# Placing anew the FFT pieces, PSUM banks and operand sums of a fused Fourier-mixing and MLP kernel

## The chip, the cores and the metric

The kernel runs on one core of a Trainium2 chip. The metric is the device time of one execution in microseconds (us); of several executions the median is taken. Five engines work at once, each through its own list of instructions: TensorE (PE) multiplies, VectorE (DVE) and ScalarE (ACT) work element by element, GpSimd (POOL) and SyncE (SP) mostly issue DMA transfers here. An instruction that must wait holds up all that stands behind it on its engine.

## The reference

Eight sequences of 3008 tokens by 256 channels are filtered in the frequency domain, and each token then goes through an MLP with a parametric ReLU.

```python
X = np.fft.rfft(x, axis=1)                  # x: (8, 3008, 256)
Y = X * (filt_r + 1j * filt_i)[None]        # 1505 frequencies x 256
y = np.fft.irfft(Y, n=3008, axis=1).reshape(24064, 256)

h = y @ moe_w_in                            # 256 -> 2048
g = np.maximum(h, 0.0) + moe_alpha * np.minimum(h, 0.0)
return g @ moe_w_out                        # 2048 -> 256, float32
```

## The kernel before

**The Fourier part.** 3008 is 47 x 64, and each transform is done as two small transforms with twiddle factors between them, all as matmuls in fp16. Per batch there are four kinds of pieces:

- 16 a pieces (`piece_a`, matmul at L211): x, loaded in four chunks by GpSimd (L170), against a 47-point table; ScalarE takes the result to `asb`, and SyncE stores it to DRAM (L216) and reads it back transposed as `at` (`turn_a`).
- 12 b pieces (`piece_b`, L231): two matmuls of 256 columns into one PSUM bank; VectorE multiplies that bank twice with the filter, into `ww` (L234) and `uu` (L235), and two DMAs of GpSimd add the halves of `ww`, swapped, onto `uu` (L237).
- 12 c pieces (`piece_c`, L249): two matmuls of `uu`, which ScalarE takes to `v` (L281). After every third one `turn_c` has SyncE write `v` to DRAM in four DMAs (L258); after the last it also issues the first three loads of the transposed `zt` (L267).
- 16 d pieces (`piece_d`, L274): four matmuls of 94 columns from `zt`, which ScalarE takes to `yT`, the MLP's input.

The first batch is done before the main loop with other, wider pieces; only 12 of its turns (`piece_t`, L352) and 12 of its d pieces are spread over the loop's start. Its filter multiplications use a filter without the sign and swap that later batches need; these are made in the loop by `neg` on VectorE (L626) and by `swapped` on GpSimd's DMA queue (L630).

All pieces of the later batches share two PSUM banks, the tiles `psF`. The string `BANKS` has one digit for each piece, in the order in which they are issued, and says which of the two it takes. A piece can only start when its bank has been emptied by the engine that reads the earlier piece in it.

**The MLP.** Batches are taken in four pairs. A pair has twelve blocks, eleven of 512 tokens and one, the sixth, of 384, so there are 48 blocks. A block has 16 steps; `step` is 16 x block + j. A step does, in this order: `flush()` (what the last block's end left to VectorE and SyncE), the operand sums due at this step (`ahead`), the pieces due at it (`plan`), `settle()` (VectorE's second half of the activation, L685), `blk.up(j)` (two matmuls of 512 columns for one 128-wide slice of the hidden layer, L498; after each second one ScalarE copies 1024 columns to `gtb`, L506, and VectorE forms the negative part, L509), and as many down matmuls of the blocks before as `LAG` lets through. So everything on TensorE is in one hand-made order, and the down products of block n run from step 16n + 18 on.

A plain block (`eight()`, L537) does 16 matmuls of 256 columns for each 128 tokens, evicts with ScalarE (L542) and stores with SyncE (L467). A block in `FAST` (`seven()`, L559) does its 2 x 2 block product with seven multiplications in place of eight: 112 matmuls of 128 columns, seven to each step. They need sums of the hidden layer's quarters a11, a12, a21, a22 and of the weights. `combine` makes the weights' sums once, at `STEPS_K`, into `tw_s` (L669 to L677). The hidden layer's are made by `Block.sums(w, h)`, h being the first or the second half of the slices:

- w = 1: z1 = a21 + a22, on VectorE (L518), into `ss`
- w = 2: z2 = z1 + a11, on VectorE (L520)
- w = 3: a21 += a11, by an accumulating DMA of GpSimd (L524, `gtb<-gtb` in the profile)
- w = 4: a12 += z2, by such a DMA (L524, `gtb<-ss`)
- w = 5 and w = 6: what 3 and 4 do, but by VectorE (L526)

Each entry of `SUMS` and `TAIL` is (step after 16n, w, h). A fast block uses `SUMS` if it lies before block 39 and the block ahead of it in order is plain, and `TAIL` otherwise. The products come in the order a12, a11, a22, z2, z1, a21, a12; the sixth begins near 16n + 29.4, the last, which reads a12 + z2, near 16n + 31.7.

**The steps.** `STEPS_A` to `STEPS_D` give the steps of the pieces of the batches from 4 on, counted from 96 (b - 1); `FIRST` gives them for batches 1 to 3. `STEPS_T` and `STEPS_E` are the first batch's turns and d pieces, `STEPS_F` and `STEPS_N` the swaps and negations of the filter, `STEPS_K` the weights' sums, `STEPS_X` and `STEPS_Q` the loads of x.

Of the kernel before, what the change touches and what calls it, by code (L numbers as in the profile page):

```python
# [19 lines left out]
DFF = 2048  # L20
NH = 32
BANKS = (
    "010101010101010101010101010101001010010110010010101010101010100101001010010101010101010100101010"
    "101010101010101010101001010101001011010101011010110110101101010101010101101001011010101101010010"
    "101101010011010101101010101010101010110010101010101101001000101001010101010101010101010101010110"
    "101010101011010010010101101010101010101010101010101010010101101010110100100010100101010101010101"
    "01010101010101101010101101001110101010101010101010101010"
)
STEPS_A = (-84, -81, -77, -76, -65, -59, -58, -58, -56, -53, -52, -51, -50, -48, -46, -43)
STEPS_B = (-21, -15, 4, 6, 13, 21, 25, 27, 32, 40, 54, 55)  # L30
STEPS_C = (2, 10, 16, 19, 24, 33, 35, 46, 62, 63, 70, 70)
STEPS_D = (89, 89, 90, 91, 92, 94, 95, 98, 100, 101, 105, 113, 118, 125, 144, 147)
STEPS_T = (0, 0, 2, 2, 13, 17, 19, 21, 21, 35, 40, 43)
STEPS_E = (6, 6, 7, 11, 23, 27, 29, 29, 53, 54, 55, 56)
STEPS_N = (24, 29, 35, 40)
STEPS_F = (20, 16, 22, 28, 34)
STEPS_K = (118, 121, 128, 133, 144)
STEPS_X = ((20, 27, 42, 52), (107, 109, 113, 126))
STEPS_Q = (-28, -18, -8, -3, 1, 9, 15, 23)
FIRST = (  # L40
# [12 lines left out]
)  # L53
FAST = frozenset((8, 10, 12, 14, 16, 18, 20, 22, 24, 26, 28, 30, 32, 34, 36, 38, 40, 42, 43, 44, 45))
SUMS = ((9, 1, 0), (10, 3, 0), (16, 2, 0), (17, 1, 1), (17, 3, 1), (19, 2, 1), (20, 4, 0), (21, 6, 1))
TAIL = ((13, 1, 0), (13, 3, 0), (18, 1, 1), (18, 3, 1), (18, 2, 0), (18, 2, 1), (20, 4, 0), (21, 4, 1))
LAG = 17
AF = mybir.ActivationFunctionType
OP = mybir.AluOpType

# [41 lines left out]
def kernel(  # L102
# [377 lines left out]
    class Block:  # L480
        def __init__(self, n, p, t0, tn):
            self.n, self.p, self.t0, self.tn = n, p, t0, tn
            self.fast = n in FAST
            self.sent = 0
# [132 lines left out]
    def put(step, fn, *args):  # L617
        plan.setdefault(step, []).append((fn, args))

    for i in range(12):  # L620
        ev = both[i % 2] if i < 4 else (on_dve, on_act)[i // 8]
        put(STEPS_T[i], f0.piece_t, 4 + i, ev)
        put(STEPS_E[i], f0.piece_d, 4 + i, ev)

# [6 lines left out]

    put(STEPS_F[0], lambda: nc.gpsimd.dma_start(out=twi_s[64:128], in_=twx_s[64:128]))
    for i in range(4):
        put(STEPS_F[1 + i], swapped, 6 * i, 6 * i + 6)
        put(STEPS_N[i], neg, 6 * i, 6 * i + 6)
    for b in range(1, NB):
        p = 96 * (b - 1)
        f = Fft(b)
        steps_a, steps_b, steps_c, steps_d = FIRST[b - 1] if b < 4 else (STEPS_A, STEPS_B, STEPS_C, STEPS_D)
        for i in range(16):  # L640
# [3 lines left out]
        if b + 1 < NB:  # L644
            for c in range(4):
                if b < 3:
                    put(STEPS_X[b - 1][c], load_x, b + 1, c)
                else:
                    for h in range(2):
                        put(p + STEPS_Q[2 * c + h], load_x, b + 1, c, (h,))  # L650
        quarters, later = (4, 1) if b < 3 else (1, 4)
# [27 lines left out]
    for n in range(5):  # L679
        put(STEPS_K[n], combine, n)  # L680
    owed = []
# [8 lines left out]
    for n, (p, t0, tn, _) in enumerate(blocks):  # L690
        old, blk = blk, Block(n, p, t0, tn)
        if blk.fast:
            for at, w, h in SUMS if n < 39 and n - 1 not in FAST else TAIL:
                ahead.setdefault(16 * n + at, []).append((blk, w, h))
        for j in range(16):
# [9 lines left out]
            blk.up(j)  # L705
            while todo and done < (step - LAG) / 16:
                try:
# [41 lines left out]
```

## Time and profile before

| what | us |
|---|---|
| median of 3 runs | 778.01 |
| lowest and highest of them | 777.71, 780.72 |
| own time of the profiled execution | 778.49 |
| its span in the profile | 776.7 |
| PE busy | 759.6 (98%) |
| VectorE busy | 691.0 (89%) |
| ScalarE busy | 606.1 (78%) |
| GpSimd busy | 264.7 (34%) |

The profile has one row for each group of instructions: line and engine, operation, written and read tiles with their shapes, the count, then busy time and mean duration, then the idle time just before them and what ended it. A row of the timeline has the start and the length of one or several instructions in a row, and in brackets the idle time ahead of them and what released them. A matmul's end in the trace is modelled, so rows of TensorE overlap; its starts are measured.

### The profile page before, as it was taken

How to read it: one execution, taken by the hardware profiler on the slowest of the kernel's cores; microseconds unless marked ns; L12 is line 12 of the kernel's file. 1: busy time of each engine (PE TensorE's matmuls, PEld its weight loads, DVE VectorE, ACT ScalarE, POOL GpSimd, SP SyncE). 2: the span in 40 equal slices, each digit the busy share in tenths (PEclk: the TensorE clock that was granted, in tenths of full speed). 3: DMA queues.
4: the chain of work that ended last, by engine and by line, in shares of the span. 5: the costliest groups of instructions: out<-in, count | busy, mean ns of one | idle time of the engine just before them, and what ended most of it. 6: DMA issues, size and time to landing. Idle time of an engine off the chain costs nothing.

```text
span 776.7 us, 18287 instructions
## 1 busy us (share of the span) xinstructions
PE 759.6 (98%) x6952; PEld 541.9 (70%) x6952; DVE 691.0 (89%) x1517; ACT 606.1 (78%) x902; POOL 264.7 (34%) x351
## 2 busy tenths in 40 slices
PE   7899999999999999999999999999999999999998
PEld 6756667666676767766677767767677777777776
DVE  3788996799999999999899999989999999989994
ACT  4687678888788887888878888788878777787773
POOL 6830641144234342353233422434222333103210
PEclk9999999999999999999999999999999999999999
DMA  9996858666997679886797869966786645635642
GB/s 181 191 191 185 163 110 209 185 130 138 192 201 153 125 162 189 207 151 129 162 196 151 156 136 178 210 134 131 161 191 153 127 86 103 167 84 105 129 96 68
DMA packets 112879, 118.74 MB, mean 153 GB/s; under 512 B 12616, under 2 KB 94296, under 8 KB 112792
## 3 DMA queue, kind: packets, MB, share of 16 engines
q0 software_dynamic: 32656, 47.99, 38.4%
q1 hardware_dynamic: 79992, 69.52, 33.7%
q8 instruction: 54, 0.88, 0.5%
q14 instruction: 33, 0.27, 0.1%
q10 hardware_dynamic: 144, 0.07, 0.0%
HBM read 56.06 MB, written 46.66 MB: 132 GB/s over the span
## 4 chain that ended last, share of the span: by engine, by line
PE 87%; DVE 4%; DMA 4%; ACT 3%; issue 1%; POOL 1%; SPq 1%; DVEq 0%; ACTq 0%; POOLq 0%
PE hps L498 38%; PE op L537 20%; PE op L559 16%; PE psF L211 3%; PE psF L274 3%; PE psF L249 2%; PE psF L231 2%; ACT gtb L506 2%; DMA twf_s<-c_twf 1%; DVE m L509 1%; DVE gtb L685 1%; DMA zt<-v_dram 1%; PE op L592 1%; DVE ww L234 1%; DVE uu L235 1%
## 5 line engine op out<-in xcount | busy, mean ns | idle before, releaser
L506 ACT ACTIVATE gtb<-hps 128x1024 f16<-128x1024 f32 (+1 forms) x384 | 385.9, 1005 | 110.5 <-PE hps L498 106.5
L498 PE MATMUL hps<-yT,win_s 128*128 128x512 f16 (+1 forms) x1536 | 449.2, 374 | 0.0
L509 DVE TENSOR_SCALAR m<-gtb,alm_s 128x512 f16<-128x512 f16 (+1 forms) x768 | 235.1, 348 | 45.4 <-ACT gtb L506 43.7
L685 DVE TENSOR_TENSOR gtb<-gtb,m 128x1024 f16<-128x1024 f16 (+1 forms) x384 | 260.9, 679 | 14.2
L537 PE MATMUL op<-wout_s,gtb 128*128 128x256 f16 x1600 | 243.1, 272 | 0.0
L237 POOL DMA_DIRECT2D uu<-ww x168 | 142.2, 1014 | 263.1 <-DVE uu L235 165.2
L537 PEld LDWEIGHTS <-gtb 128*128 128x128 f16 x1600 | 156.0, 98 | 104.6
L498 PEld LDWEIGHTS <-win_s 128*128 128x128 f16 x1536 | 136.7, 98 | 25.6 <-issue 2.5
L559 PEld LDWEIGHTS <-gtb 128*128 128x128 f16 x1680 | 114.3, 98 | 53.8 <-DMA gtb<-ss 1.0
L524 POOL DMA_DIRECT2D gtb<-gtb x42 | 40.5, 963 | 192.9 <-DVE ss L518 62.1
L559 PE MATMUL op<-wout_s,gtb 128*128 128x128 f16 x1008 | 85.1, 219 | 1.1 <-ACT gtb L506 0.6
L281 ACT ACTIVATE asb<-psF 96x512 f16<-96x512 f32 x112 | 65.1, 594 | 9.7 <-PE psF L211 8.4
L281 ACT ACTIVATE yT<-psF 128x376 f16<-128x376 f32 x120 | 56.2, 486 | 10.5 <-PE psF L274 9.3
L559 PEld LDWEIGHTS <-ss 128*128 128x128 f16 x672 | 47.1, 98 | 23.3
L170 POOL DMA_DIRECT2D xs<-in_x_dram x64 | 54.4, 1014 | 14.2 <-PE psF L211 13.4
L559 PE MATMUL op<-tw_s,gtb 128*128 128x128 f16 x672 | 58.1, 219 | 0.0
L559 PE MATMUL op<-tw_s,ss 128*128 128x128 f16 x672 | 58.0, 219 | 0.0
L234 DVE TENSOR_TENSOR ww<-psF,filts_s 128x512 f16<-128x512 f32 x84 | 57.4, 684 | 0.3 <-PE psF L231 0.2
L235 DVE TENSOR_TENSOR uu<-psF,filt_s 128x512 f16<-128x512 f32 x84 | 57.2, 681 | 0.0
L281 ACT ACTIVATE v<-psF 128x512 f16<-128x512 f32 x84 | 49.0, 598 | 7.8 <-PE psF L249 7.2
L211 PE MATMUL psF<-xs,wf_s 94*96 94x512 f16 x112 | 41.2, 380 | 1.4 <-ACT yT L281 0.4
L274 PE MATMUL psF<-wi_s,zt 96*128 96x94 f16 x504 | 39.4, 205 | 2.2 <-ACT yT L281 1.4
(86 smaller groups left out, 524.9 us busy)
## 6 DMA issues: line engine op xcount, KB each, us to landing
out_dram<-osb SPq DMA_DIRECT2D x127, 128.0 KB
xs<-in_x_dram POOLq DMA_DIRECT2D x64, 188.0 KB, 5.8
a_dram<-asb SPq DMA_DIRECT2D x28, 384.0 KB
uu<-ww POOLq DMA_DIRECT2D x168, 64.0 KB, 3.0
v_dram<-v SPq DMA_DIRECT2D x112, 96.0 KB
zt<-v_dram SPq DMA_DIRECT2D x28, 384.0 KB
gtb<-gtb POOLq DMA_DIRECT2D x42, 256.0 KB, 4.5
at<-a_dram SPq DMA_DIRECT2D x20, 384.0 KB
```

The costliest lines, as they stand in the source:

```text
L211: nc.tensor.matmul(ps[0:96], wf1_s, xs[:, o : o + 512], start=True, stop=True)
L234: nc.vector.tensor_mul(ww, px, filts_s[:, 2 * kp : 2 * kp + 2])
L235: nc.vector.tensor_mul(uu, px, filt_s[:, 2 * kp : 2 * kp + 2])
L237: nc.gpsimd.dma_start(out=uu[o : o + 64], in_=ww[64 - o : 128 - o], accum_op=OP.add)
L274: nc.tensor.matmul(ps[:, m], self.zt[g][:, 4 * mh + m, dh * 128 : dh * 128 + 128], wi3_s, start=True, stop=True)
L281: nc.scalar.activation(o, i, AF.Copy)
L498: nc.tensor.matmul(self.hps[:, j % 2, 0:tn], win_s[:, kt, j * 128 : (j + 1) * 128], yT[:, kt, self.t0 : self.t0 + tn], start=(kt == 0), st ...
L506: nc.scalar.activation(g, hs, AF.Copy)
L509: nc.vector.tensor_scalar(ms[:, i], g[:, i], 0.0, a, OP.min, OP.mult)
L537: nc.tensor.matmul(op[:, si % 2], self.pair(k // 2)[:, k % 2, 128 * si : 128 * si + 128], wout_s[:, k], start=(k == 0), stop=(k == 15))
L559: nc.tensor.matmul(acc[:, 128 * i : 128 * i + 128], x[:, k, 128 * i : 128 * i + 128], b[:, k], start=first and k + i == 0, stop=k == 7, sk ...
L685: nc.vector.tensor_add(g, g, ms)
```

## The change

All step tables, the digits of `BANKS` and the two lists of sums are written anew; blocks 9 and 11 take the place of 8 and 10 among the fast ones, so there are 21 of them as before. `LAG` becomes 17.0, the same number. No function changes. In `SUMS` the second halves of the third and the fourth sum both go by VectorE (w = 5 and 6) at 16n + 24 and 16n + 28; before, only the fourth's second half did, at 16n + 21, and the third's went by DMA at 16n + 17. With 11 fast, block 12 follows a fast block and so uses `TAIL`: fifteen blocks use `SUMS` and six `TAIL`, where it was sixteen and five.

```diff
 BANKS = (
-    "010101010101010101010101010101001010010110010010101010101010100101001010010101010101010100101010"
...
+    "010101010101010101010101010101001101010101001010101010101010100100101001010010011010100101101010"
...
-STEPS_A = (-84, -81, -77, -76, -65, -59, -58, -58, -56, -53, -52, -51, -50, -48, -46, -43)
-STEPS_B = (-21, -15, 4, 6, 13, 21, 25, 27, 32, 40, 54, 55)
-STEPS_C = (2, 10, 16, 19, 24, 33, 35, 46, 62, 63, 70, 70)
-STEPS_D = (89, 89, 90, 91, 92, 94, 95, 98, 100, 101, 105, 113, 118, 125, 144, 147)
-STEPS_T = (0, 0, 2, 2, 13, 17, 19, 21, 21, 35, 40, 43)
-STEPS_E = (6, 6, 7, 11, 23, 27, 29, 29, 53, 54, 55, 56)
-STEPS_N = (24, 29, 35, 40)
-STEPS_F = (20, 16, 22, 28, 34)
-STEPS_K = (118, 121, 128, 133, 144)
-STEPS_X = ((20, 27, 42, 52), (107, 109, 113, 126))
-STEPS_Q = (-28, -18, -8, -3, 1, 9, 15, 23)
+STEPS_A = (-84, -82, -77, -75, -65, -63, -58, -57, -56, -54, -52, -52, -50, -48, -46, -43)
+STEPS_B = (-21, -12, 4, 8, 14, 22, 26, 26, 34, 40, 53, 55)
+STEPS_C = (2, 11, 16, 20, 24, 32, 35, 47, 61, 63, 70, 70)
+STEPS_D = (89, 90, 91, 93, 94, 94, 97, 99, 102, 104, 106, 114, 118, 121, 145, 147)
+STEPS_T = (0, 0, 2, 2, 13, 17, 19, 20, 22, 34, 37, 43)
+STEPS_E = (6, 6, 7, 9, 23, 27, 27, 29, 51, 56, 56, 58)
+STEPS_N = (24, 27, 30, 56)
+STEPS_F = (14, 6, 18, 25, 48)
+STEPS_K = (104, 114, 123, 126, 131)
+STEPS_X = ((18, 22, 57, 76), (89, 114, 120, 147))
+STEPS_Q = (-42, -23, -14, -3, 3, 10, 12, 27)
 FIRST = (
-    ((8, 10, 15, 16, 16, 17, 19, 20, 22, 22, 24, 25, 26, 28, 28, 30),
-     (41, 41, 45, 45, 49, 54, 58, 63, 65, 65, 71, 72),
-     (48, 50, 52, 58, 60, 62, 69, 70, 71, 73, 77, 80),
-     (94, 94, 95, 95, 96, 102, 102, 105, 105, 107, 108, 111, 119, 120, 120, 129)),
+    ((9, 10, 12, 16, 16, 18, 20, 21, 21, 24, 25, 26, 26, 28, 28, 31),
+     (41, 41, 45, 46, 51, 53, 58, 60, 62, 64, 69, 74),
+     (48, 50, 54, 59, 60, 61, 66, 69, 72, 73, 76, 81),
+     (94, 94, 95, 95, 97, 98, 99, 100, 103, 103, 106, 109, 119, 119, 120, 123)),
...
 )
-FAST = frozenset((8, 10, 12, 14, 16, 18, 20, 22, 24, 26, 28, 30, 32, 34, 36, 38, 40, 42, 43, 44, 45))
-SUMS = ((9, 1, 0), (10, 3, 0), (16, 2, 0), (17, 1, 1), (17, 3, 1), (19, 2, 1), (20, 4, 0), (21, 6, 1))
-TAIL = ((13, 1, 0), (13, 3, 0), (18, 1, 1), (18, 3, 1), (18, 2, 0), (18, 2, 1), (20, 4, 0), (21, 4, 1))
-LAG = 17
+FAST = frozenset((9, 11, 12, 14, 16, 18, 20, 22, 24, 26, 28, 30, 32, 34, 36, 38, 40, 42, 43, 44, 45))
+SUMS = ((9, 1, 0), (12, 2, 0), (13, 3, 0), (18, 1, 1), (20, 2, 1), (20, 4, 0), (24, 5, 1), (28, 6, 1))
+TAIL = ((13, 1, 0), (13, 3, 0), (19, 1, 1), (20, 2, 0), (21, 3, 1), (22, 2, 1), (23, 4, 0), (26, 4, 1))
+LAG = 17.0
```

In the program that results, TensorE has the same 6952 matmuls of the same forms, VectorE 30 sums at L526 where it had 16, and GpSimd 54 DMAs at L524 (27 of each kind) where it had 68 (42 and 26).

More of the change, by code (lines that the diff above doesn't have):

```diff
@@ L22 @@
 BANKS = (
-    "010101010101010101010101010101001010010110010010101010101010100101001010010101010101010100101010"
[L24 to L27, printed above, removed]
-)
-STEPS_A = (-84, -81, -77, -76, -65, -59, -58, -58, -56, -53, -52, -51, -50, -48, -46, -43)
@@ L40 @@
-FIRST = (
[12 rows of a table removed]
-)
-FAST = frozenset((8, 10, 12, 14, 16, 18, 20, 22, 24, 26, 28, 30, 32, 34, 36, 38, 40, 42, 43, 44, 45))
-SUMS = ((9, 1, 0), (10, 3, 0), (16, 2, 0), (17, 1, 1), (17, 3, 1), (19, 2, 1), (20, 4, 0), (21, 6, 1))
-TAIL = ((13, 1, 0), (13, 3, 0), (18, 1, 1), (18, 3, 1), (18, 2, 0), (18, 2, 1), (20, 4, 0), (21, 4, 1))
-LAG = 17
+    "010101010101010101010101010101001101010101001010101010101010100100101001010010011010100101101010"
+    "101010101010101010101010101010101010010101010110011010100101001010101010010100100101010010101010"
@@ new lines @@
+    "101010100010101010101010101010101010100101001010100101010101101001010101010010101010101010101010"
+    "101001010101010101011010010101010100101010101010101010101010010101010101010110100101010101001010"
+    "10101010101010101010101010101001010101010101010101010101"
+)
+STEPS_A = (-84, -82, -77, -75, -65, -63, -58, -57, -56, -54, -52, -52, -50, -48, -46, -43)
+STEPS_B = (-21, -12, 4, 8, 14, 22, 26, 26, 34, 40, 53, 55)
+STEPS_C = (2, 11, 16, 20, 24, 32, 35, 47, 61, 63, 70, 70)
+STEPS_D = (89, 90, 91, 93, 94, 94, 97, 99, 102, 104, 106, 114, 118, 121, 145, 147)
```

16 rows, old and new, of the table FIRST are left out of this document.

## The prediction

> **What bounds the kernel now.** I read the page's busy shares, the groups by line, and then, because one number decides everything, the matmul timeline from start to start.
>
> ```profile
> span 776.7 us, 18287 instructions
> PE 759.6 (98%) x6952; PEld 541.9 (70%) x6952; DVE 691.0 (89%) x1517; ACT 606.1 (78%) x902; POOL 264.7 (34%) x351
> ```
>
> TensorE is busy for 98% of the span and nothing else comes near it but VectorE (89%). The page says that a busy PE is not PE at its peak, so I do not take the remaining 2% for the stalls, but work out how long its matmuls need when they follow each other without a wait.
>
> ```profile
> 38.82 0.59 PE L498 MATMUL hps<-yT,win_s 128*128 128x512 f16 x2
> ...
> 137.39 0.59 PE L498 MATMUL hps<-yT,win_s 128*128 128x512 f16 x2
> 137.82 0.60 PE L537 MATMUL op<-wout_s,gtb 128*128 128x256 f16 x4
> 138.26 0.59 PE L498 MATMUL hps<-yT,win_s 128*128 128x512 f16 x2
> ...
> 187.92 0.55 PE L559 MATMUL op<-wout_s,gtb 128*128 128x128 f16 x7
> 188.31 0.59 PE L498 MATMUL hps<-yT,win_s 128*128 128x512 f16 x2
> ...
> 771.51 1.95 PE L592 MATMUL hps<-wout_s,gtb 128*128 128x128 f16 x32
> ```
>
> From start to start, two matmuls of 512 columns take 0.43 us (137.39 to 137.82), four of 256 take 0.44 and seven of 128 take 0.39, so 0.215, 0.110 and 0.056 each; by columns one of 94 takes 0.041. The bars overlap: 0.59 is shown where the next begins after 0.43, so a wait that a row shows in brackets costs 0.16 us more than the bracket. The main loop runs from 38.82 to 771.51 + 1.95 = 773.46, that is 734.6 us.
>
> ```profile
> L498 PE MATMUL hps<-yT,win_s 128*128 128x512 f16 (+1 forms) x1536 | 449.2, 374 | 0.0
> L537 PE MATMUL op<-wout_s,gtb 128*128 128x256 f16 x1600 | 243.1, 272 | 0.0
> L559 PE MATMUL op<-wout_s,gtb 128*128 128x128 f16 x1008 | 85.1, 219 | 1.1 <-ACT gtb L506 0.6 <-DVE gtb L685 0.5
> L559 PE MATMUL op<-tw_s,gtb 128*128 128x128 f16 x672 | 58.1, 219 | 0.0
> L559 PE MATMUL op<-tw_s,ss 128*128 128x128 f16 x672 | 58.0, 219 | 0.0
> L211 PE MATMUL psF<-xs,wf_s 94*96 94x512 f16 x112 | 41.2, 380 | 1.4 <-ACT yT L281 0.4 <-DMA filts_s<-filt_s 0.3 <-DVE zt L284 0.3
> L274 PE MATMUL psF<-wi_s,zt 96*128 96x94 f16 x504 | 39.4, 205 | 2.2 <-ACT yT L281 1.4 <-DVE uu L235 0.4 <-DMA zt<-v_dram 0.3
> ```
>
> Counts by pitch: L498 1408 x 0.215 and, for the four short blocks, 128 x 0.161, together 323; L537 1600 x 0.110 = 176; L559 2352 x 0.0557 = 131; L211 24; L274 inside the loop 496 x 0.041 = 20; pieces b and c (7 batches x 12 x 4 matmuls by the code) 336 x 0.110 = 37; the twelve turns of the first batch and the last block 10. That makes 721, so some 13 us of the loop are stalls; adding up the gaps of the matmul timeline itself gives 12.6, which I use since pitches are rounded. This is the ceiling of any gain: the change does not touch a matmul, so 38.8 us before and 3.3 us after the loop and the 721 inside stay.
>
> **What the change removes.** These are the stalls whose cause I can follow into the new order.
>
> ```profile
> 80.45 0.39 PE L352 MATMUL psF<-id,v 128*96 128x128 f16 x2 [0.47 <-DVE uu L235]
> 90.52 0.39 PE L249 MATMUL psF<-uu,twi_s 128*128 128x256 f16 x2 [0.59 <-DMA uu<-ww]
> 111.35 0.38 PE L249 MATMUL psF<-uu,twi_s 128*128 128x256 f16 x2 [0.40 <-ACT asb L281]
> 150.40 0.34 PE L274 MATMUL psF<-wi_s,zt 96*128 96x94 f16 x4 [0.38 <-DVE uu L235]
> 189.69 0.23 PE L559 MATMUL op<-wout_s,gtb 128*128 128x128 f16 x1 [0.46 <-DVE gtb L685]
> 242.03 0.33 PE L274 MATMUL psF<-wi_s,zt 96*128 96x94 f16 x4 [0.28 <-ACT yT L281]
> 321.66 0.33 PE L274 MATMUL psF<-wi_s,zt 96*128 96x94 f16 x4 [0.40 <-ACT yT L281]
> 375.35 0.38 PE L211 MATMUL psF<-xs,wf_s 94*96 94x512 f16 x1 [0.41 <-ACT yT L281]
> 499.81 0.38 PE L274 MATMUL psF<-wi_s,zt 96*128 96x94 f16 x5 [0.28 <-DMA zt<-v_dram]
> 506.70 0.28 PE L559 MATMUL op<-wout_s,gtb 128*128 128x128 f16 x2 [0.62 <-ACT gtb L506]
> ```
>
> - 80.45 (0.63 with the 0.16): a turn of the first batch waits for a bank that VectorE must empty, with a negation (L626) of step 40 in its way; that goes to step 56. Half, 0.3.
> - 90.52 (0.75): the third c piece of batch 1 at step 52, its `uu` still in flight; it moves to 54. Gone.
> - 111.35 (0.56): the eighth, due at 70 with its b at 63; now 69 and 60. Gone.
> - 150.40, 242.03, 321.66, 375.35 (0.54, 0.44, 0.56, 0.57): the bank asked for is the one last filled, right behind a b piece or another d piece. With the digits of `BANKS` redrawn, the instruction order has only one pair of pieces in the loop that asks for a bank under 0.5 us of matmul work after its predecessor (four before). Gone, 2.1.
> - 189.69 (0.62): the first product of the first fast block, block 8, behind VectorE, which had just made the last twisted weight (L677). The weights move to steps 104 to 131 and the first fast block is 9. Gone.
> - 499.81 (0.44): `zt` is late beside a sum's DMA, and sums by DMA become fewer. Half, 0.2.
> - 506.70 (0.78): the product's a12 += z2 came by a DMA that stood on POOL behind the other sum and a `uu`; it is now at 24 and 28 by VectorE in these blocks. Gone.
>
> Sum 0.3 + 0.75 + 0.56 + 2.1 + 0.62 + 0.2 + 0.78 = 5.3 us. The other 7.3 us are single waits of a few tenths which I can't place; I take them as staying alike, with bounds of 2.4 less (a third) and 2.4 more.
>
> **What it adds.** The sums first.
>
> ```profile
> L526 DVE TENSOR_TENSOR gtb<-gtb,ss 128x1024 f16<-128x1024 f16 x16 | 11.0, 685 | 0.0
> L524 POOL DMA_DIRECT2D gtb<-gtb x42 | 40.5, 963 | 192.9 <-DVE ss L518 62.1 <-PE hps L498 57.0 <-DVE m L509 41.5
> gtb<-gtb POOLq DMA_DIRECT2D x42, 256.0 KB, 4.5
> gtb<-ss POOLq DMA_DIRECT2D x26, 256.0 KB, 6.1
> 478.20:492.60 14.40, 14.40 (x111) 9.94 (x109) 12.92 (x29) 10.01 (x13) 2.40 (x4) 1.00 0.96 195
> 521.80:537.40 15.60, 15.60 (x166) 11.21 (x164) 15.19 (x34) 13.72 (x23) 8.29 (x11) 1.00 0.83 162
> ```
>
> Sixteen blocks had one VectorE sum each (L526). Now fifteen have two, for six blocks (12 is one now) use the other list, which stays with DMAs: 30 instead of 16, and 54 DMAs instead of 68. Each sum takes 0.685 us by its bar, some 0.60 from start to start as VectorE's bars overlap like PE's, so 14 x 0.60 = 8.4 us more VectorE work in total, 0.6 in each such block; and POOL issues 14 x 0.96 less. Is that 0.6 covered? The rows of windows (columns: stretch, PE, PEld, VectorE, ScalarE, POOL, clock, DMA share) show both kinds of block: in 521.80:537.40 VectorE is busy 15.19 of 15.60 us and PE loses nothing, so VectorE may be full without holding TensorE; in 478.20:492.60 it has 1.48 us to spare. The new sums stand at 16n+24 and 28, in the second half of the plain block behind the fast one, and by the order of VectorE's instructions the fullest blocks (25, 31, 37) end up with one or two operations less and the block behind them with two or three more, so the load evens out. I put the sums at nothing; the work that hides them is TensorE's own, and without it they would cost up to 8.4, which is the rival below. The gain from fewer DMAs: a sum's DMA lands 4.5 to 6.1 us after its issue, a VectorE sum is ready after 0.7.
>
> In a sentence of its own: the Trainium skill, "DMA: Bandwidth & Descriptors", section "Anatomy of one DMA — SWDGE (gpsimd) path", gives 2.0 us plus bytes over 436e3, by which, as an estimate, 256 KB would take 2.6 us; the rows above say 4.5 and 6.1, so here the measurement decides, and by the page the wait at 506.70 would not have been the transfer's and the gain 0.78 less.
>
> **A wait that is new.** In batch 1 the last c piece goes from 80 to 81, and with it `turn_c` from 81 to 82. That moves its four DMAs on SP behind three stores (L467) of the block evicted at 123.84.
>
> ```profile
> 122.76 2.88 SPq L258 DMA_DIRECT2D v_dram<-v  x4
> 129.16 1.25 SPq L267 DMA_DIRECT2D zt<-v_dram  x3
> 130.50 2.35 SPq L467 DMA_DIRECT2D out_dram<-osb  x3
> ...
> 123.84 0.59 ACT L542 ACTIVATE osb<-op 128x512 f32<-128x512 f32 x1
> ...
> 133.83 0.50 PE L274 MATMUL psF<-wi_s,zt 96*128 96x94 f16 x8
> ```
>
> Now: `v` is issued from 122.76 to 125.64, has landed 3.52 later (129.16, where the `zt` loads go out), and the first d piece runs at 133.83 without a bracket, so `zt` takes 4.67 or less. After: the stores wait for the eviction, 124.43; three take 2.35, to 126.78; four `v` 2.88, to 129.66; landing 3.52, to 133.18; `zt` up to 4.67, to 137.85, against a piece that stays at step 94: 4.0 late. With every issue at the 0.42 of the `zt` loads (1.25 / 3) and `zt` landing in 3.52 it is 124.43 + 1.25 + 1.67 + 3.52 + 3.52 = 134.39, 0.6 late. I take 2.5, nearer to the measured issues. Everything on PE stands behind that piece, so it is paid in full.
>
> The loads of x and the swaps of the filter (72 DMAs) move too, some by 30 steps and past sums and `uu` on POOL; POOL is free for two thirds of the span, and the closest load stands 10 steps (some 9 us, 734.6 us being 768 steps) ahead of its first a piece. Nothing.
>
> Small things, a b piece 7 us before its c, the negation at 56 behind its DMA of step 48, two fast products close behind their last VectorE operation: 0.8, between 0 and 2.
>
> **The sum.** -5.3 + 2.5 + 0.8 = -2.0. The profiled execution took 778.49 by its own time (776.7 span and 1.8 around it), 0.5 above the median of 778.01; I apply the difference to the median: 776.0. By bounds: -5.3 - 2.4 + 0.6 = -7.1 at one end, -5.3 + 2.4 + 4.0 + 2.0 = +3.1 at the other, 770.9 to 781.1.
>
> **Rivals.**
> - *The redrawn plan cleans up more than I can name.* A third of the unplaced waits goes, and step 94 costs 0.6: 778.0 - 5.3 - 2.4 + 1.4 = 771.7. For it: the pieces that ask for a bank early fall from 24 to 12 in the order. Against it: most unplaced waits stand in the first ten blocks, whose plan gets no looser.
> - *VectorE becomes the bound.* It decides where a stretch like 521.80:537.40 gets a sum more than its 0.41 us of slack holds: from there `ww`, `uu` and the activation's products come later block after block, the banks come free later, and TensorE waits. At most all 8.4 us: 778.0 - 5.3 + 2.5 + 0.8 + 8.4 = 784.4. For it, the 15.19 of 15.60; against it, that neighbouring stretches leave over 1 us each.
> - *The clock drops at step 94.* The trace shows it once, ahead of the loop:
>
> ```profile
> 18.00:21.00 3.00, 1.13 (x13) 0.76 (x11) 1.33 (x2) 1.60 (x4) 2.90 (x7) 1.00 0.99 192
> 21.00:24.00 3.00, 2.50 (x19) 2.21 (x20) 2.97 (x4) 0.90 (x2) 3.00 (x6) 0.62 1.14 245
> ```
>
> After a stretch with TensorE 1.13 of 3.00 us busy the granted clock averages 0.62, that is 2.3 us at half. A stall of 4.0 at step 94 followed by such a drop costs 1.5 + 1.1 more: 778.6. The rule of the Trainium skill, "TensorE: Matmul & The Clock Gate", section "🔬 Part 1: The HAM clock gate (the "warmup" mystery)", that a window without work halves the clock, agrees with these two rows and stands behind this rival.
> - *Nothing comes of it:* the waits removed reappear at the next piece, since each only moved TensorE against the same engines: 778.0.
>
> **How the numbers follow.** The forecast, 776.0 with its own range 774.0 to 778.5, has 0.46; the clean plan 0.26; VectorE 0.15; nothing 0.08; the clock 0.05. A measurement of this kernel tells 0.5%, 3.9 us, from no change: under 774.1 is faster, over 781.9 slower. The forecast's lower tail adds 0.02 to faster, its upper bound 0.01 to slower: 0.28, 0.56, 0.16. The range takes in the clean plan and the bounds, and leaves out VectorE as the bound: 771.5 to 781.5.
>
> **What would show it.** Right: no waits of the ten kinds above at their places; a bracket of 2 to 4 us at the first d piece of batch 1 with `zt<-v_dram` as its releaser; L526 x30 and L524 27 and 27; stretches of even blocks with PE idle under 0.2. Wrong: brackets by `uu` or `ww` in the blocks 12 to 38, or fast products that wait for L526 at 28, which comes last before its product; or no wait at step 94, which would make the store's place harmless.

## The result and the profile after

The changed kernel takes 774.96 us (median of 16 runs, 773.27 to 779.09), the kernel before 779.21 us in 16 runs beside it (777.71 to 783.6). The ratio is 0.9949, 95% interval 0.9936 to 0.9962, so 4 us less. The profiled execution of the changed kernel is one of its longer ones: 776.81 us by its own time, 775.0 of span. The page's first lines, the groups of the operand sums and one issue row:

```profile
span 775.0 us, 18257 instructions
PE 758.2 (98%) x6952; PEld 541.5 (70%) x6952; DVE 692.2 (89%) x1531; ACT 604.4 (78%) x902; POOL 253.3 (33%) x337
...
L526 DVE TENSOR_TENSOR gtb<-gtb,ss 128x1024 f16<-128x1024 f16 x15 | 10.2, 680 | 0.0
L526 DVE TENSOR_TENSOR gtb<-gtb 128x1024 f16<-128x1024 f16 x15 | 10.2, 679 | 0.0
L524 POOL DMA_DIRECT2D gtb<-gtb x27 | 31.8, 1176 | 71.1 <-DVE m L509 41.9 <-DVE ss L518 22.3 <-DVE gtb L685 4.9
L524 POOL DMA_DIRECT2D gtb<-ss x27 | 26.0, 964 | 40.0 <-PE op L559 29.7 <-PE hps L498 4.7 <-DVE m L509 4.6
...
gtb<-ss POOLq DMA_DIRECT2D x27, 256.0 KB, 4.7
```

VectorE does 14 sums more and is busy for 1.2 us more, not for the 8.4 of their pitch. The busy time counts a moment in which bars overlap only once; added one by one, VectorE's bars come to 777.6 us before and 787.0 after, 9.5 more (sums over the two traces). Where the time went is seen in the busy time of the stretches of the main loop. First the kernel before (columns: stretch, PE, PEld, VectorE, ScalarE, POOL, clock, DMA share, GB/s):

```profile
100.00:167.80 67.80, 67.01 (x512) 46.45 (x510) 55.12 (x126) 55.95 (x87) 22.35 (x30) 1.00 0.68 159
167.80:310.00 142.20, 141.41 (x1241) 98.63 (x1239) 131.71 (x288) 115.54 (x170) 52.15 (x65) 1.00 0.82 168
310.00:460.00 150.00, 149.15 (x1391) 105.75 (x1388) 141.19 (x312) 124.28 (x190) 56.47 (x71) 1.00 0.77 161
460.00:620.00 160.00, 159.09 (x1479) 113.07 (x1478) 148.79 (x331) 129.27 (x194) 52.16 (x64) 1.00 0.75 160
```

Then the changed kernel in the same stretches:

```profile
100.00:167.80 67.80, 66.09 (x507) 45.71 (x504) 53.00 (x122) 55.25 (x86) 21.05 (x28) 1.00 0.72 165
167.80:310.00 142.20, 142.20 (x1245) 99.40 (x1244) 133.38 (x294) 115.90 (x172) 51.81 (x65) 1.00 0.78 163
310.00:460.00 150.00, 150.00 (x1400) 106.57 (x1399) 142.99 (x321) 124.67 (x192) 53.95 (x68) 1.00 0.74 155
460.00:620.00 160.00, 159.11 (x1491) 113.44 (x1490) 149.98 (x337) 129.62 (x195) 47.08 (x58) 1.00 0.70 152
```

From 167.8 to 460 us TensorE no longer stands still for a moment that the view shows. Ahead of that it stands still longer than before. The waits of the matmul timeline from 80 us on with a bracket over 0.2, one of them at 527.95:

```profile
80.73 0.48 PE L352 MATMUL psF<-id,v 128*96 128x128 f16 x3 [0.28 <-DVE uu L235]
89.68 0.38 PE L231 MATMUL psF<-at,twf_s 128*128 128x256 f16 x2 [0.40 <-ACT v L281]
98.45 0.38 PE L249 MATMUL psF<-uu,twi_s 128*128 128x256 f16 x2 [0.28 <-ACT yT L281]
135.55 0.51 PE L274 MATMUL psF<-wi_s,zt 96*128 96x94 f16 x8 [1.50 <-DMA zt<-v_dram]
527.95 0.38 PE L249 MATMUL psF<-uu,twi_s 128*128 128x256 f16 x2 [0.89 <-DMA uu<-ww]
```

The one at 135.55 is the wait foreseen for the first d piece of batch 1. Its chain, on SyncE and ScalarE:

```profile
124.94 2.36 SPq L467 DMA_DIRECT2D out_dram<-osb  x3
127.35 2.72 SPq L258 DMA_DIRECT2D v_dram<-v  x4
131.72 1.25 SPq L267 DMA_DIRECT2D zt<-v_dram  x3
...
124.31 0.60 ACT L542 ACTIVATE osb<-op 128x512 f32<-128x512 f32 x1
```

The `v` stores end 127.35 + 2.72 = 130.07, have landed 1.65 later, and `zt` needs 3.83 from its issue (131.72) to the matmul (135.55).

### The profile page after: what moved, and what is told of

The parts are those of the page before. It is cut to its first block, busy times and chain, and to the rows that moved or that the text cites. A ratio compares the mean times of both kernels' runs of the same rounds, so it can differ in the third digit from the quotient of the medians.

```text
span 775.0 us, 18257 instructions
## 1 busy us (share of the span) xinstructions
PE 758.2 (98%) x6952; PEld 541.5 (70%) x6952; DVE 692.2 (89%) x1531; ACT 604.4 (78%) x902; POOL 253.3 (33%) x337
## 4 chain that ended last, share of the span: by engine, by line
PE 89%; DMA 4%; DVE 3%; ACT 1%; issue 1%; POOL 1%; DVEq 0%; POOLq 0%; ACTq 0%
PE hps L498 39%; PE op L537 21%; PE op L559 17%; PE psF L211 3%; DMA twf_s<-c_twf 3%; PE psF L274 3%; PE psF L249 2%; PE psF L231 2%; DMA uu<-ww 1%; DVE gtb L685 1%; DVE m L509 1%; PE op L592 1%; POOL xs L170 1%; DMA zt<-v_dram 0%; ACT gtb L506 0%
## 5 line engine op out<-in xcount | busy, mean ns | idle before, releaser
L237 POOL DMA_DIRECT2D uu<-ww x168 | 144.4, 1036 | 358.6 <-DVE uu L235 182.0
L524 POOL DMA_DIRECT2D gtb<-gtb x27 | 31.8, 1176 | 71.1 <-DVE m L509 41.9
```

What stands on the lines that cost most here:

```text
L237: nc.gpsimd.dma_start(out=uu[o : o + 64], in_=ww[64 - o : 128 - o], accum_op=OP.add)
```

## The experiments

All ratios below are to the kernel before on the same chip, with a 95% interval. "Loss" is the bracket of a row plus the 0.16 us by which bars overlap. The clock of a run is its mean over the whole span: a value of 0.998 or below says that TensorE was at half speed for a while, but not where. In the third profile of the changed kernel (0.997) that was ahead of the loop, at 21.47 us, and not after a wait of the loop.

### The two kernels again

The changed kernel was profiled three times in all, the kernel before twice.

> The changed kernel once more, unaltered, for a second profile of it. Theory P (the gain lies in the places of pieces and banks, and the waits that are left have fixed causes): ratio to before near 0.995, and the wait of batch 1's first d piece for zt (loss 1.66 us at 135.55 in the first profile) is there again, between 1 and 3 us. Rival N (waits on transfers scatter from run to run): the c piece's wait for uu at 527.95 (loss 1.06 us) is gone or elsewhere, and the sum of the loop's gaps, 9.5 us in the first profile, differs by more than 2 us. Both can hold.

Ratio 0.9945 (0.9924 to 0.9966). The profiled execution had a span of 777.3 us. The wait for `zt` is there and longer (first row, timeline), that at 527.95 is not, and the granted clock falls after it (the two rows of windows, third number from their end):

```profile
136.21 0.70 PE L274 MATMUL psF<-wi_s,zt 96*128 96x94 f16 x8 [2.23 <-DMA zt<-v_dram]
...
132.95:136.36 3.41, 1.18 (x13) 0.74 (x11) 2.21 (x6) 1.02 (x2) 0.00 (x0) 1.00 0.92 234
136.36:139.78 3.42, 3.42 (x26) 2.44 (x25) 0.00 (x0) 1.78 (x5) 0.00 (x0) 0.50 0.92 296
```

TensorE is at half for 3.4 us, which costs 1.7. Theory P holds, and rival N in part: the place of this wait is fixed, its length is not, and waits on transfers come and go (one of 0.60 for `at` stands at 224.86 instead). The gaps of over 0.1 us from one matmul's start to the next, beyond the usual pitch, add up to 11.2 us against 9.4 in the first profile, 1.8 more where rival N asked for over 2.

> The changed kernel, unaltered, beside its variants on one chip: 0.995 of before. Theory C (the clock drops after the wait for zt in some runs only): a third or less of the runs at a mean clock of 0.998 or below.

Ratio 0.9952 (0.9934 to 0.997); one run of six at a clock of 0.998 or below, the profiled one. The wait for `zt` loses 1.60 us and no drop follows it; the drop of this run stands at 21.47, ahead of the loop, so it is none of theory C's.

> The kernel before once more, unaltered, for a second profile. Theory D (the new sums gain more than the 1.0 us that the first profile shows because the waits of the last product for its DMA sums, gtb<-ss, scatter from run to run): the waits with a fixed cause are there again (losses near 0.64, 0.75, 0.56, 0.54, 0.62, 0.45, 0.57, 0.57 us from 80 to 375 us), those at 499.81 and 506.70 (0.44, 0.79) are not, or differ, and others for gtb sums stand elsewhere. Rival F (all waits are fixed): 506.70 within 0.2 us of 0.79.

One run, 780.71 us. The waits with a fixed cause stand again within 0.1 us, but the one for `uu` at 90.52 is three times as long, and the clock falls after it:

```profile
91.01 0.39 PE L249 MATMUL psF<-uu,twi_s 128*128 128x256 f16 x2 [1.95 <-DMA uu<-ww]
...
88.81:92.22 3.41, 1.47 (x14) 0.91 (x12) 3.10 (x8) 1.47 (x2) 2.22 (x4) 1.00 0.60 120
92.22:95.64 3.42, 3.42 (x20) 1.94 (x18) 1.19 (x4) 1.99 (x3) 0.50 (x1) 0.50 0.90 132
```

Again 3.4 us at half. The waits at 499.81 and 506.70 are also there again, with losses of 0.45 and 0.72, as rival F has it; so theory D is not borne out for these two in this profile, while that for `uu` scatters as it says of the sums.

### The sums by themselves, and the places by themselves

```diff
-SUMS = ((9, 1, 0), (10, 3, 0), (16, 2, 0), (17, 1, 1), (17, 3, 1), (19, 2, 1), (20, 4, 0), (21, 6, 1))
-TAIL = ((13, 1, 0), (13, 3, 0), (18, 1, 1), (18, 3, 1), (18, 2, 0), (18, 2, 1), (20, 4, 0), (21, 4, 1))
+SUMS = ((9, 1, 0), (12, 2, 0), (13, 3, 0), (18, 1, 1), (20, 2, 1), (20, 4, 0), (24, 5, 1), (28, 6, 1))
+TAIL = ((13, 1, 0), (13, 3, 0), (19, 1, 1), (20, 2, 0), (21, 3, 1), (22, 2, 1), (23, 4, 0), (26, 4, 1))
```

put into the kernel before:

> The kernel before with SUMS and TAIL of the changed one, all else as it was: 32 sums at L526, 52 DMAs at L524. Theory P: only the wait at 506.70 (loss 0.79 us) and perhaps that at 322.62 (0.20) go, the others (150.40, 189.69, 242.03, 321.66, 375.35 and those up to 111.35) stay: ratio 0.999. Rival S: most of the gain comes with it, 0.996 or 0.997. Rival V: 1.001 or above.

Ratio 0.9964 (0.995 to 0.9977). The same lines taken back in the changed kernel:

> The changed kernel with SUMS and TAIL of the kernel before: 16 sums at L526 less one as block 12 uses TAIL, 15 in all, 69 DMAs at L524. Theory P: the places make the gain, so the ratio to before stays near 0.995 to 0.996 (0 to 1 us given back, where a product waits for a DMA sum queued behind uu). Rival S (the sums by VectorE make the gain): the ratio goes back to 0.998 or above. Rival V (the VectorE sums cost something): it falls below 0.994.

Ratio 1.0106 (1.0077 to 1.0135), 12 us over the changed kernel. Together with the two kernels themselves ("places" are all other parts of the change: step tables, `BANKS`, `FAST`):

| ratio to before | old sums | new sums |
|---|---|---|
| old places | 1 | 0.9964 |
| new places | 1.0106 | 0.9949 |

Rival S was nearer than theory P: the new sums alone bring 2.8 of the 4 us, and the new places without them lose 8. The ratios count runs with a drop of the clock too, 7 of 17 of before on this chip and 1 of 12 with the new sums. Of the runs at a clock above 0.998 alone, the spans have medians of 776.65 (before) and 774.8 (new sums in old places): 1.85 us, so about a third of the 2.8 is the clock, and that the new sums make drops rarer is not shown.

Most of the waits that come in the second case are those of products for their sums, 6.0 us of loss in all (the longest, in the timeline of the changed kernel with the old sums); another 4.2 us are six waits of pieces for a bank that VectorE empties (released by its `uu`):

```profile
322.35 0.34 PE L559 MATMUL op<-tw_s,gtb 128*128 128x128 f16 x3 [0.54 <-DMA gtb<-gtb]
325.14 0.28 PE L559 MATMUL op<-wout_s,gtb 128*128 128x128 f16 x2 [1.50 <-DMA gtb<-ss]
...
511.84 0.28 PE L559 MATMUL op<-wout_s,gtb 128*128 128x128 f16 x2 [2.99 <-DMA gtb<-ss]
```

### Which sum it is

The second half of the third sum alone goes back to a DMA, at 16n + 18:

```diff
-SUMS = ((9, 1, 0), (12, 2, 0), (13, 3, 0), (18, 1, 1), (20, 2, 1), (20, 4, 0), (24, 5, 1), (28, 6, 1))
+SUMS = ((9, 1, 0), (12, 2, 0), (13, 3, 0), (18, 1, 1), (18, 3, 1), (20, 2, 1), (20, 4, 0), (28, 6, 1))
```

> The changed kernel with the second half of the third sum by DMA at 16n+18 in place of VectorE at 16n+24 (15 sums at L526, 69 DMAs at L524); the fourth's stays on VectorE at 28. Theory D (a DMA sum queued on POOL between uu transfers comes late for its product or makes uu late): 1 to 3 us more than the changed kernel, 0.997 to 0.999, with waits for gtb<-gtb, gtb<-ss or uu in the profile. Rival E (what hurts in the old lists under the new places is only the fourth sum's early VectorE step or the TAIL): 0.995, as the changed kernel.

Ratio 0.9997 (0.9982 to 1.0011): 3.7 us of the gain depend on this one sum. Six of its 12 runs are at a clock of 0.998 or below; the spans of the other six have a median 1.0 us below that of such runs of before, where the changed kernel's were 3.65 and 3.2 below, so without drops the sum is worth 2.2 to 2.7. Two views of it, first POOL, then the matmul timeline:

```profile
312.68 0.85 POOL L524 DMA_DIRECT2D gtb<-gtb  x1 [2.50 <-PE op L559]
313.23 0.85 POOL L170 DMA_DIRECT2D xs<-in_x_dram  x1
313.76 1.21 POOL L524 DMA_DIRECT2D gtb<-ss  x1
```

```profile
320.94 0.34 PE L559 MATMUL op<-tw_s,gtb 128*128 128x128 f16 x3 [0.70 <-DMA gtb<-gtb]
323.90 0.29 PE L559 MATMUL op<-wout_s,gtb 128*128 128x128 f16 x2 [1.68 <-DMA gtb<-ss]
507.03 0.28 PE L559 MATMUL op<-wout_s,gtb 128*128 128x128 f16 x2 [0.97 <-DMA gtb<-ss]
```

The third sum's transfer is issued at 312.68 and its product released at 320.94, 8.3 us later; the fourth's first half, which stands behind it and a load of x, is issued at 313.76 and its product released at 323.90, 10.1 later. In the changed kernel the third sum's second half does not stand on POOL there, and the product of the fourth runs without a wait:

```profile
312.24 0.86 POOL L524 DMA_DIRECT2D gtb<-ss  x1 [0.59 <-PE op L559]
...
321.98 0.28 PE L559 MATMUL op<-wout_s,gtb 128*128 128x128 f16 x2
```

This transfer too takes long, 9.7 us to its landing at 321.92, and is in time by 0.06 us. The variant is 0.80 us ahead in its order of matmuls at this place (the same one starts at 310.70 and 311.50), so its transfer goes out 313.76 + 0.80 - 312.24 = 2.3 us later and takes 0.4 longer (10.1 in place of 9.7). At the other wait, 507.03, where the variant is 1.79 us behind, it goes out 3.5 us later by the same reckoning (499.81 - 1.79 - 494.52) and lands faster, after 7.2 us in place of 8.9. So what makes the fourth sum late is its place on POOL, behind a transfer that itself stood there 2.50 us waiting, and not a slower transfer. The VectorE sum is worth more by the transfer that it takes out of the way of the others (losses of 1.84 and 1.13) than by its own speed (0.86).

### How much room VectorE has

```diff
-(12, 2, 0), (13, 3, 0), (18, 1, 1), (20, 2, 1), (20, 4, 0), (24, 5, 1), (28, 6, 1)
+(12, 2, 0), (13, 5, 0), (18, 1, 1), (20, 2, 1), (20, 6, 0), (24, 5, 1), (28, 6, 1)
```

> The changed kernel with the first halves of the third and fourth sum by VectorE too in the fifteen blocks with SUMS (same steps): 60 sums at L526 and 24 DMAs at L524, 18 us more work on VectorE. Theory P (VectorE has room): ratio within 0.002 of the changed kernel's 0.995. Rival V (VectorE sets the pace where it is 97% busy): up to 18 us more, 1.018; half of it, 1.006, would say that part of the blocks are bound by it.

Ratio 0.9999 (0.9983 to 1.0015): 3.9 us over the changed kernel for 30 more sums, 0.13 each where their own time is 0.60. That is over the 0.002 that theory P allowed and far from the 18 us of rival V. The 0.13 is what is left after 30 transfers less on POOL, so it is no price of VectorE's work alone: six waits of TensorE for a bank that VectorE empties lose 3.0 us in this profile, while the wait for `uu` at 527.95 is gone and that for `zt` is 0.58. The stretch 310 to 460 shows VectorE 146.20 of 150.00 busy and TensorE 0.87 short:

```profile
310.00:460.00 150.00, 149.13 (x1389) 105.46 (x1388) 146.20 (x327) 124.11 (x190) 42.98 (x55) 1.00 0.61 131
```

### The wait for zt

`turn_c` of batch 1's last quarter is issued in the step of its last c piece, ahead of the three stores:

```diff
-                put(p + steps_c[kp] + 1, f.turn_c, kp // 3)
+                put(p + steps_c[kp] + (b > 1 or kp < 11), f.turn_c, kp // 3)
```

> The changed kernel with batch 1's last turn_c issued in the step of its last c piece (81) instead of the next (82), so that its four v stores stand on SP ahead of the three output stores. Theory P: zt goes out some 2.4 us earlier, the wait at 135.55 (1.66 us) goes, and the ratio is 0.002 below that of the unaltered changed kernel (0.993 against 0.995). Rival: the v transfers wait for the last c piece's eviction on ScalarE anyway and the output stores now come later, so that a store tile comes free later: no difference, within 0.001.

Ratio 0.9934 (0.9914 to 0.9955), and once more:

> The changed kernel with batch 1's last turn_c in the step of its last c piece, once more. Theory P: 0.0010 to 0.0020 below the unaltered changed kernel on the same chip, the wait for zt at 133 under 0.6 us, no run at a clock of 0.998 or below. Rival: no difference over 0.0005, as the loss only moves.

Ratio 0.9938 (0.9916 to 0.9961), beside 0.9952 for the unaltered one on that chip. The medians are 0.8 and 0.9 us lower (774.27 against 775.09, 774.43 against 775.33), about half of the 1.6 first expected, within the 0.0010 to 0.0020 of the second time; the intervals overlap, so two times the same sign is all that the times say. The profiles say why it is not more. The two executions, the first two rows of the one and the last two of the other:

```profile
122.43 2.21 SPq L258 DMA_DIRECT2D v_dram<-v  x4
129.56 1.25 SPq L267 DMA_DIRECT2D zt<-v_dram  x3
...
122.25 2.42 SPq L258 DMA_DIRECT2D v_dram<-v  x4
130.43 1.25 SPq L267 DMA_DIRECT2D zt<-v_dram  x3
```

`v` is issued by 124.64 and 124.67, more than 5 us earlier than in the changed kernel, but takes 4.9 and 5.8 us to land where it took 1.65. The wait for `zt` loses 0.45 and 1.28 us where it lost 1.66, 2.39 and 1.60, so the second expectation's wait under 0.6 and no run with a drop did not come. Of 13 runs one is at a clock of 0.998 or below, against 7 of 29 of the unaltered changed kernel; where in most of these runs the drops stood is not known.

In the other direction, `turn_c` six steps later, behind another store:

```diff
-                put(p + steps_c[kp] + 1, f.turn_c, kp // 3)
+                put(p + steps_c[kp] + (7 if b == 1 and kp == 11 else 1), f.turn_c, kp // 3)
```

> The changed kernel with batch 1's last turn_c issued at step 88 instead of 82, so that on SP it stands behind the store of another a chunk and goes out some 2 us later. Theory C (a wait of TensorE over about 2.2 us halves the clock for some 3.4 us: 2.39 us did so in the second profile of the changed kernel, 1.66 us did not in the first): the wait at 135 grows to 3.5 to 5 us, the granted clock is at half for 3 to 4 us after it in the profile, and the ratio is 0.995 + (2.5 + 1.7) / 779 = 1.000. Rival (the clock drop was chance): the wait grows but the clock stays 1.00: 0.998.

Ratio 0.9973 (0.996 to 0.9986), by the ratios 1.9 us over the changed kernel. The wait grew to a loss of 2.95, less than expected, and the clock did not fall after it in the profiled execution:

```profile
132.30:135.72 3.42, 1.52 (x12) 0.98 (x10) 2.46 (x7) 1.48 (x2) 0.00 (x0) 1.00 0.46 147
135.72:139.13 3.41, 2.52 (x30) 2.06 (x31) 0.00 (x0) 1.91 (x5) 0.00 (x0) 1.00 0.96 257
```

Six of its 12 runs have a clock of 0.998 or below; their spans have a median of 776.9 us, those of the other six 773.95. Theory C falls as it was put: losses of 2.11 and 2.39 were followed by a drop, one of 2.95 was not, nor was one of 3.15, the last row of the timeline with the old sums above. The traces say what decides. Where a profile has two drops, their starts lie a whole multiple of 3.413 us apart (in the second profile of the changed kernel 136.36 and 778.07, 188 times). So stretches of 3.413 us can be counted back from any drop, here from the one after the loop's end at 774.01, and the two rows above are cut so. The stall of 2.95 falls on two of them and leaves TensorE 1.52 and 2.52 us of work; the losses of 2.11 and 2.39 fell into one each and left 1.47 and 1.18 (the rows above), and half clock followed from that stretch's end. The loss of 3.15 with the old sums is split too:

```profile
507.39:510.80 3.41, 1.46 (x20) 1.02 (x16) 2.71 (x8) 2.32 (x6) 0.00 (x0) 1.00 1.13 215
510.80:514.21 3.41, 2.37 (x27) 1.76 (x28) 0.28 (x1) 1.06 (x2) 0.00 (x0) 1.00 0.95 248
```

With 1.46 us of work left no drop came here, with 1.47 one did, so these traces place the bound near 1.5 us of 3.41 and no closer. That longer waits make drops more frequent fits this, but six runs of 12 against 7 of 29 do not show it, as the clock of a run does not tell where it fell.

### Two smaller parts of the change

Blocks 8 and 10 fast in the changed kernel:

> The changed kernel with blocks 8 and 10 fast in place of 9 and 11 (block 12 then uses SUMS). Theory P: the weights' sums now end at step 131, long before block 8's first product at 146, so only small waits move: within 0.001 of the changed kernel, 0.994 to 0.996. Rival W (the choice of 9 and 11 spares POOL and VectorE where batch 2's and 3's pieces crowd): 1 to 3 us more, 0.996 to 0.999.

Ratio 0.9982 (0.9965 to 1), 0.003 over the unaltered one on that chip (0.9952), 2.7 us by the medians: rival W. In its profile VectorE is full from 220 to 230 us and TensorE stands still for 1.8 us there, in two waits; in the changed kernel (last row) nothing is lost:

```profile
220.00:230.00 10.00, 8.18 (x90) 5.71 (x88) 9.97 (x23) 5.62 (x9) 4.16 (x5) 1.00 0.77 186
...
221.81 0.38 PE L231 MATMUL psF<-at,twf_s 128*128 128x256 f16 x2 [0.75 <-DMA v_dram<-v]
229.23 0.34 PE L274 MATMUL psF<-wi_s,zt 96*128 96x94 f16 x4 [1.07 <-DMA zt<-v_dram]
```

```profile
220.00:230.00 10.00, 10.00 (x76) 6.79 (x75) 9.54 (x22) 6.61 (x8) 3.51 (x4) 1.00 0.76 189
```

The longer of the two is for a transfer (`zt`), and the first names one as well, though not one that a b piece reads, so its cause is open. That VectorE's full load makes them is not shown: in the changed kernel it is busy for 9.54 us of the same 10. Block 12 goes back to the list `SUMS` with it, so this is the price of the blocks and of that list together.

And one place alone, in the kernel before: batch 1's third c piece at 54 in place of 52, behind two d pieces of the first batch and just ahead of the b piece of step 54. The digits of `BANKS` keep their order, so the two d pieces swap their banks.

```diff
-     (48, 50, 52, 58, 60, 62, 69, 70, 71, 73, 77, 80),
+     (48, 50, 54, 58, 60, 62, 69, 70, 71, 73, 77, 80),
```

> The kernel before with one edit: batch 1's third c piece at step 54 in place of 52, as the changed kernel has it. It waits for uu at 90.52, with losses of 0.75, 0.98 and 2.11 us in three profiles, the last with a clock drop. Theory P: the wait goes, ratio 0.998 to 0.999, and fewer runs at a clock of 0.998 or below than the 7 of 29 of before. Rival (the wait moves to the next piece, since POOL and VectorE are behind there anyway): 1.000.

Ratio 1.0002 (0.9986 to 1.0018), the number of the rival. The wait for `uu` is gone and the b piece behind it waits for its bank:

```profile
91.27 0.38 PE L231 MATMUL psF<-at,twf_s 128*128 128x256 f16 x2 [0.66 <-ACT yT L281]
```

It asks for the bank that, with the swap, the second d piece has filled two pieces earlier (90.06) and that ScalarE has to empty. So the rival's reason, that POOL and VectorE are behind, is not what this row shows, and how the c piece would do at 54 with the d pieces' banks kept was not tried. Four of its 12 runs are at a clock of 0.998 or below, no fewer than with the kernel before (7 of 24 on this chip). In this profile the products of the kernel before wait longer for their sums than in the first: a loss of 0.91 at 322.46, where it was 0.20 and 0.45 in the two profiles of before, and 0.86 at 506.81.

## Why the prediction was right, and where it was not

The time lay in the range and moved the way that was forecast, with 1.0 us between 776.0 and 774.96; as a ratio, 0.9974 was forecast (776.0 / 778.01) and 0.9949 measured. So 2 of the 4 us were not foreseen, and that 776.0 came so near is partly luck: the median of before that it started from, 778.01 of three runs, is 1.2 us below that of 16. By its steps:

- *TensorE and its stalls are the bound, about 12.6 us the ceiling.* Right: the loop less its gaps of over 0.1 us (from start to start) is 724.0 to 724.7 us in every profile, and the gaps, 6.4 to 18.7 us, set the time.
- *The ten waits.* Right for the four bank waits, those at 111.35, 189.69, 499.81 and 506.70, none of which stands in the three profiles of the changed kernel; that at 80.45 is down from a loss of 0.63 to 0.44. At 90.52 the wait for `uu` is gone and a b piece's wait for a bank of 0.56 stands at 89.68: the fourth rival for this one wait, and in the third c piece's experiment a b piece comes to wait as well. That at 189.69 is gone with blocks 8 and 10 fast too, so the weights' earlier steps remove it and not the choice of the blocks. What the prediction missed at 90.52 is that the wait is also one that pulled the clock down.
- *"I put the sums at nothing", but for 0.78 at 506.70.* The step that failed. The new lists alone are worth 2.8 us (0.9964; 1.85 without the runs with a drop), and 3.7 us of the gain fall when one sum goes back to a DMA (2.2 to 2.7 without). The term that was mis-sized is the transfer's: the prediction counted the single wait that one profile showed, while waits on sums differ from profile to profile (0.20, 0.45, 0.91 at one place; 1.0, 1.2 and 2.4 us in all in the three profiles with the old lists in the old places). It also took a transfer's price as its own wait, where the one put back holds up the sum behind it on POOL.
- *Blocks 9 and 11.* Counted with 0.6 for the wait at 189.69; together with block 12's list they are worth 2.7, of which 1.8 is the stall between 220 and 230 us in the profile. The prediction had no term for it. Why the old choice makes transfers late there is open.
- *The wait at step 94.* Right in place and chain: the `v` stores ended at 130.07 where 129.66 was worked out for a loop half a us ahead. Its size, 2.5 within 0.6 to 4.0, was 1.66, 2.39 and 1.60; the landing of `v` was the part off, 1.65 against the 3.52 taken.
- *Small things, 0.8, and the 7.3 us left as they were.* The small things were not tried one by one. Among the waits taken as unchanged, those of blocks 0 and 1 grew: from their first matmul to block 2's they take 31.34 us where they took 30.36, 1.0 more, or more in every profile with the new places.
- *The rivals.* VectorE as the bound was wrong in size: thirty further sums cost 0.13 each net of the transfers that they replace, not 0.60, though not nothing. The clean plan needed only 0.6 us at step 94, which took 1.6 to 2.4. The clock rival was right as an occasional cost: in one of three profiles, 3.4 us at half, 1.7 lost. Its two rows at 18 to 24 us, with TensorE busy for 1.13 of 3.00, do not show a window without work; as the stretches of 3.413 us say, a mostly idle one was enough.

No single part carries the change alone. Which of the step tables beyond those tried make the rest is open; the new places lose 8 us under the old lists and win 1 under the new ones (0.9964 against 0.9949, intervals that touch), so places and sums can't be priced one by one.

The changed kernel with the early `turn_c` has the lowest ratios here, 0.9934 and 0.9938.

## What to carry to other kernels

When a loop's order is laid out by hand against queues, price a change of the order and a change of what stands in the queues together: here the new places alone would have been judged a loss of 8 us. A wait on a transfer seen once in a profile is a sample: look at a second profile before taking its length as the gain of removing it. And a transfer taken off an engine that issues in order is worth what it held up behind it, which can be more than its own wait.

## What was not expected of the hardware

- Losses of 2.11 and 2.39 us on TensorE were each followed by 3.4 us at half clock, those of 1.66, 2.95 and 3.15 were not. The Trainium skill, "TensorE: Matmul & The Clock Gate", section "🔬 Part 1: The HAM clock gate (the "warmup" mystery)", has the clock halved after an idle window of some 3.4 us that runs free of the program. The traces agree with the length, 3.41 us at half, and with a window that runs free: drops of one profile start a whole multiple of 3.413 us apart, and the losses of 2.95 and 3.15 were split between two such windows. That the window must be idle from end to end they do not bear out: with 1.47 and 1.18 us of work in it the clock still fell.
- The same four `v` stores landed 1.65 us after their last issue when issued late, and 4.9 and 5.8 us when issued 5 us earlier beside other transfers (packets of the loads of x ran until 126.98 us in the first of these).
